# Attention and gated MLP, one core: every transpose of the attention weights takes all 128 rows of its tile

## The chip, the cores and the metric

The kernel runs on one core of one Trainium2 chip. The metric is the device time of one execution in microseconds (us), the median of several runs.

## The reference

Eight batches of eight heads, 576 tokens, head size 64, so 64 heads in all; then a feed-forward part with spatial gating on each batch.

```python
scores = scale * np.matmul(q, k.transpose(0, 1, 3, 2))
cum = np.cumsum(np.maximum(s, 0.0), axis=-1)
bias = -(cum[:, :, :, None] - cum[:, :, None, :])
scores = np.where(causal, -1000000000.0, scores + np.minimum(bias, 0.0))
attn = np.exp(scores - np.max(scores, axis=-1, keepdims=True))
attn = attn / (np.sum(attn, axis=-1, keepdims=True) + 1e-09)
x = np.matmul(attn, v)                 # then [batch, token, 512]
...
h = gelu(x @ w_in)                     # 1024 wide, halves u and v
v_n = layer_norm(v) * g_ln
v_s = np.einsum('ts,bsd->btd', w_sg, v_n) + b_sg[None, :, None]
out = x + (u * v_s) @ w_out
```

Everything above the diagonal of the attention weights is zero.

## The kernel before

**Attention, one head.** The 576 query tokens are cut into five tiles of rows: tile 0 has 64 rows (tokens 0 to 63), tiles 1 to 4 have 128 each and start at tokens 64, 192, 320 and 448 (`IT0`, `ITR`). Only columns up to the tile's last token are computed (`ITW` = 64, 192, 320, 448, 576). `scores` issues the score matmuls (`qk_part`, lines 287 to 290), the masked copy from PSUM with its running minimum on VectorE (`ttr`, line 297), the exponential on ScalarE (`exp_`, line 307) and the division by the row sums (`norm`, line 321, on GpSimd; for the first twelve heads tile 3's is on VectorE). The results are the SBUF tiles p_0 to p_4; two sets of them (`pbuf`) serve even and odd heads. Columns right of `ITW` up to the padded width `PW` are cleared once at the start and stay zero.

`transposes` then turns these weights, 128 key columns at a time, into PSUM. A transpose is a TensorE matmul whose stationary operand is the block of p and whose moving operand is the identity `ident`, all fp32 (line 362, in one place 402). It goes through four banks of PSUM a head, taken from the pool `ps_pt` of two buffers:

- bank A, key tokens 0 to 127: tiles 3, 2, 1 and 0;
- bank B, tokens 256 to 383 for tiles 2, 3 and 4, and tile 4's tokens 0 to 127;
- bank C, tokens 128 to 255: tiles 1 to 4;
- bank D, tokens 384 to 511 for tiles 3 and 4, and tile 4's last 64 tokens.

In each of the banks B, C and D one tile meets the diagonal with half its rows: its first 64 rows hold only zeros there. For this block `half=True` transposes rows 64 to 127 alone, that is a 64-row block that starts at partition 64. Tile 0 has 64 rows anyway. So each head has five transposes of 64 rows (one in each of A, B and C, two in D) and ten of 128.

After each bank the PSUM tile is copied out by `evac`: from head 12 on as a high part (ScalarE, a rounding copy at line 85) and a low part (VectorE, the rest, line 90), pah and pal and so on; before that as one plain copy (line 374). `pv` multiplies these with the values (lines 438, 443, 455; its first bank x0 also comes from `ps_pt`).

**Feed-forward.** `ffn` runs for one batch while the next batch's heads are in work: matmuls at lines 494 (vm), 556 (um), 571 to 575 (sm) and 590 (om), each sum of products of high and low parts.

**Order.** Each step has a place on an axis counted in heads, and steps are issued by place. The framework's scheduler then lays the instructions of every engine in an order of its own, so neighbours on a queue are its choice.

Of the kernel before, what the change touches and what calls it, by code (L numbers as in the profile page):

```python
# [8 lines left out]
F32 = mybir.dt.float32  # L9
# [5 lines left out]
ALU = mybir.AluOpType  # L15
# [5 lines left out]
P = 128  # L21
# [10 lines left out]
ITR = [64, 128, 128, 128, 128]  # L32
ITW = [64, 192, 320, 448, 576]
PW = [128, 256, 384, 512, 576]
# [22 lines left out]
def tile_attn_gmlp(  # L57
# [12 lines left out]
    nc = tc.nc  # L70
# [9 lines left out]
    def eng(key):  # L80
        return [{"s": nc.scalar, "g": nc.gpsimd, "v": nc.vector}[x] for x in ENG[key]]
# [10 lines left out]
    heads = {}  # L92
# [25 lines left out]
            with later():  # L118
                nc.sync.dma_start(out=d["vr"], in_=vp[h])

# [1 line left out]
    dram = ctx.enter_context(tc.tile_pool(name="dram", bufs=1, space=bass.MemoryType.DRAM))  # L122
    cum = dram.tile([2, BH, S], F32, name="cum")
    st = moe.tile([P, 5, BH], F32, name="st", tag="vt", bufs=2)
# [9 lines left out]
    for c0, n in ((0, 512), (512, REM)):  # L134
        ps = ps_sc.tile([P, 512], F32, name="cps", tag="sc")
# [14 lines left out]
    split(cc[0:BH, 0, :], cc[0:BH, 1, :], cf[0:BH, :], nc.scalar, nc.gpsimd)  # L150
    nc.sync.dma_start(out=cum.rearrange("a h s -> h a s"), in_=cc[0:BH].bitcast(F32))

# [1 line left out]
    ident = const.tile([P, P], F32, name="ident")  # L154
    nc.vector.memset(ident, 0.0)
    nc.gpsimd.affine_select(out=ident, in_=ident, pattern=[[1, P]], base=0, channel_multiplier=-1,
# [5 lines left out]
    half = const.tile([P, 1], F32, name="half")  # L162
    nc.vector.memset(half, -0.5)
    g_b = const.tile([P, DH], F32, name="g_b")

# [1 line left out]
    q2 = []  # L167
    pbuf = []
    sums = []
    for i in range(2):  # L170
        t = const.tile([66, S], F32R, name=f"q2_{i}")
        nc.vector.memset(t[64:66, :].bitcast(F32), 1.0)
        q2.append(t)
        ts_ = []
        for it in range(5):
            t = const.tile([P, PW[it]], F32, name=f"p_{i}_{it}")
            if PW[it] > ITW[it]:
                nc.gpsimd.memset(t[:, ITW[it]:PW[it]], 0.0)
            ts_.append(t)
        pbuf.append(ts_)  # L180
        t = const.tile([P, 5], F32, name=f"sum_{i}")
        nc.vector.memset(t, 1.0)
        sums.append(t)

# [1 line left out]
    wi = const.tile([P, NC, 2, DFF], F32R, name="wi")  # L186
    wo = const.tile([P, NC, 2, DM], F32R, name="wo")
    ws = const.tile([P, NT, 2, S], F32R, name="ws")
# [69 lines left out]
                part(wide, w_out[c * P:(c + 1) * P, fs], wo[:, c, 0, fs], wo[:, c, 1, fs])  # L258
                yield 1

# [1 line left out]
    xr = {}  # L262

    def split_head(h):
# [17 lines left out]
    def qk_part(h, it, pst, c0, j0, j1):  # L282
        d = heads[h]
        i0, r = IT0[it], ITR[it]
        o = pst[0:r, c0:c0 + j1 - j0]
        if h < NQ:
            nc.tensor.matmul(o, d["q"][:, i0:i0 + r], d["k"][:, j0:j1], start=True, stop=True)  # L287
            return
        nc.tensor.matmul(o, d["q1"][:, i0:i0 + r], d["k1"][:, j0:j1], start=True, stop=False)  # L289
        nc.tensor.matmul(o, q2[h % 2][:, i0:i0 + r], d["k2"][0:66, j0:j1], start=False, stop=True)  # L290

    def ttr(h, it, pst, c0, j0, j1, first):
        d = heads[h]
        r = ITR[it]
        m0 = 448 + 128 - ITW[it] if it else 448
        mn = d["mn"]
        nc.vector.tensor_tensor_reduce(  # L297
            out=pbuf[h % 2][it][0:r, j0:j1], in0=pst[0:r, c0:c0 + j1 - j0],
            in1=mask[0:r, m0 + j0:m0 + j1], scale=-0.125,
            scalar=3.0e38 if first else mn[0:r, it:it + 1],  # L300
            op0=ALU.add, op1=ALU.min, accum_out=mn[0:r, it:it + 1])
# [6 lines left out]
                             accum_out=sums[h % 2][0:r, it:it + 1])  # L308

    def norm(h, its, rs):  # L310
        c = slice(its[-1], its[0] + 1)
        nc.vector.tensor_scalar(out=rs[:, c], in0=sums[h % 2][:, c], scalar1=1e-9, scalar2=None, op0=ALU.add)
        nc.vector.reciprocal(out=rs[:, c], in_=rs[:, c])  # L313
        for it in its:
            r, w = ITR[it], ITW[it]
            p = pbuf[h % 2][it][0:r, 0:w]
            e = eng("n0" if h < NP else "n")[it]
            if e is nc.scalar:
                nc.scalar.activation(out=p, in_=p, func=AF.Copy, scale=rs[0:r, it:it + 1])
            else:  # L320
                e.tensor_scalar(out=p, in0=p, scalar1=rs[0:r, it:it + 1], scalar2=1.0, op0=ALU.mult, op1=ALU.mult)  # L321

    def scores(h):
        d = heads[h]
        d["mn"] = att.tile([P, 5], F32, name="mn", tag="mn")
        t = ps_sc.tile([P, 512], F32, name="sc", tag="sc")
        qk_part(h, 3, t, 0, 0, 448)
        qk_part(h, 0, t, 448, 0, 64)
        ttr(h, 3, t, 0, 0, 448, True)
        exp_(h, 3)  # L330
        ttr(h, 0, t, 448, 0, 64, True)
        exp_(h, 0)
        yield 0.5
        t = ps_sc.tile([P, 512], F32, name="sc", tag="sc")
        qk_part(h, 2, t, 0, 0, 320)
        qk_part(h, 1, t, 320, 0, 192)
        ttr(h, 2, t, 0, 0, 320, True)
        exp_(h, 2)
        ttr(h, 1, t, 320, 0, 192, True)
        exp_(h, 1)  # L340
        yield 0.5
        rs = att.tile([P, 5], F32, name="rs", tag="rs")
        norm(h, (3, 2, 1, 0), rs)
        t = ps_sc.tile([P, 512], F32, name="sc", tag="sc")
        qk_part(h, 4, t, 0, 0, CH)
        ttr(h, 4, t, 0, 0, CH, True)
        t = ps_sc.tile([P, 512], F32, name="sc", tag="sc")
        qk_part(h, 4, t, 0, CH, S)
        ttr(h, 4, t, 0, CH, S, False)
        exp_(h, 4)  # L350
        yield 0.6
        norm(h, (4,), rs)
        yield 0.1

    def transposes(h):
        d = heads[h]
        pb = pbuf[h % 2]
        pt = {}

        def tr(ps, c, it, jb, half=False):  # L360
            a, r = (64, 128) if half else (0, ITR[it])
            nc.tensor.transpose(out=ps[:, c:c + r - a], in_=pb[it][a:r, jb:jb + P], identity=ident[a:r, a:r])  # L362

        def new(name, w):
            if h < NP:
                x = "hl"[h % 2]
                pt[name] = (att.tile([P, w], F32, name=name + x, tag=name + x, bufs=1),)
            else:
                pt[name] = tuple(att.tile([P, w], F32R, name=name + x, tag=name + x, bufs=1) for x in "hl")

        def evac(name, c0, ps, w, e=nc.scalar):
            if h < NP:
                o = pt[name][0][:, c0:c0 + w]
                (e.copy if e is nc.scalar else e.tensor_copy)(out=o, in_=ps[:, 0:w])  # L374
            else:
                hi, lo = (t[:, c0:c0 + w] for t in pt[name])
                split(hi, lo, ps[:, 0:w], nc.scalar, nc.vector)

        d["pt"] = pt
        t = ps_pt.tile([P, 512], F32, name="pt", tag="pt")  # L380
        for it in (3, 2, 1, 0):
            tr(t, IT0[it], it, 0)
        new("pa", 896)
        evac("pa", 0, t, 448)
        yield 0.43
        t = ps_pt.tile([P, 512], F32, name="pt", tag="pt")
        tr(t, 128, 2, 256, True)
        tr(t, 192, 3, 256)
        tr(t, 0, 4, 0)
        tr(t, 320, 4, 256)  # L390
        evac("pa", 448, t, 448, nc.vector)
        yield 0.43
        t = ps_pt.tile([P, 512], F32, name="pt", tag="pt")
        tr(t, 0, 1, 128, True)
        for it in (2, 3, 4):
            tr(t, 128 * it - 192, it, 128)
        new("pb", 448)
        evac("pb", 0, t, 448)
        yield 0.43
        t = ps_pt.tile([P, 512], F32, name="pt", tag="pt")  # L400
        tr(t, 0, 3, 384, True)
        nc.tensor.transpose(out=t[0:64, 192:256], in_=pb[4][64:128, 512:576], identity=ident[64:128, 64:128])
        tr(t, 64, 4, 384)
        new("pd", 192)
        if h < NP:
            pe = att.tile([P, 64], F32, name="pe", tag="pe", bufs=1)
            nc.vector.tensor_copy(out=pe[0:64, :], in_=t[0:64, 192:256])
            evac("pd", 0, t, 192, nc.vector)
        else:
            pe = att.tile([P, 64], F32R, name="pe", tag="pe", bufs=1)  # L410
            hi, lo = pt["pd"]
            nc.scalar.copy(out=pe[0:64, :], in_=t[0:64, 192:256])
            nc.scalar.copy(out=hi, in_=t[:, 0:192])
            nc.vector.tensor_tensor(out=pe[64:128, :], in0=t[0:64, 192:256], in1=pe[0:64, :].bitcast(F32),
                                    op=ALU.subtract)
            nc.vector.tensor_tensor(out=lo, in0=t[:, 0:192], in1=hi.bitcast(F32), op=ALU.subtract)
        d["pe"] = pe
        yield 0.35

# [45 lines left out]
        del heads[h]  # L465
        yield 0.5

# [1 line left out]
    def ffn(b):  # L469
        xs = []  # L470
        for c in range(NC):
# [128 lines left out]
        for w in (ORD0 if b == 0 else ORDL if b == B - 1 else ORDER).split():  # L600
            yield from unit[w[0]](int(w[1]), int(w[2:] or 0))

# [1 line left out]
    steps = []  # L604
    tick = count()

# [3 lines left out]
    def advance(g, h):  # L610
        if h not in g[1]:
            g[1][h] = g[0](h)
        next(g[1][h], None)

    sc, tr, pp = (scores, {}), (transposes, {}), (pv, {})
    for h in range(BH):
        if h > 0:
# [79 lines left out]
```

## Time and profile before

| | us |
|---|---|
| median of 3 runs | 873.3 |
| lowest and highest run | 872.01, 875.57 |
| span of the profiled execution, first to last instruction | 869.9 |
| PE busy in it | 849.2 |
| DVE, POOL, ACT busy | 671.3, 567.6, 562.3 |
| weight loads (PEld) busy | 713.6 |

Of the profiled execution the page gives the span; the median of the runs lies 3.4 us above it, the lowest run 2.1 us. PE is TensorE's matmuls, PEld its weight loads, which go beside matmuls. A matmul's row begins when it reads its first data, and its end is modelled; rows of neighbouring matmuls overlap, so the distance from one start to the next tells what one costs, not the length of a row. In a row such as `64*128 64x128` the part with the star is rows*columns of the stationary operand.

### The profile page before, as it was taken

The page shows a single profiled execution, that of the slowest core. Times are in us where ns is not written, and L with a number is a line of the kernel's source. Part 1 is how long each engine was busy: PE and PEld are TensorE (multiplying, and loading weights), DVE is VectorE, ACT ScalarE, POOL GpSimd, SP SyncE. Part 2 cuts the span into 40 slices and gives each one's busy share as a digit, 9 for nine tenths or more (in the row PEclk, how much of TensorE's full clock was granted, in tenths as well). Part 3 has the DMA queues.
Part 4 walks back from the last instruction along what each step waited for, and adds up shares of the span by engine and source line. Part 5 has one row for each costly group of instructions (what it writes and reads, how often), then busy time and mean ns, then how long its engine had stood idle before and what let it go on. Part 6 is the DMA issues. An engine that isn't in the chain of part 4 may idle for free.

```text
span 869.9 us, 17259 instructions
## 1 busy us (share of the span) xinstructions
PE 849.2 (98%) x5341; PEld 713.6 (82%) x5341; DVE 671.3 (77%) x2041; ACT 562.3 (65%) x1544; POOL 567.6 (65%) x885
## 2 busy tenths in 40 slices
PE   6899899999999999999999999999999999999988
PEld 3455567988889888898889988889888988899888
DVE  5998778866798678975899668976789668984662
ACT  4677567766687566865677567875668657872340
POOL 4978747767478557685667666786576855773441
PEclk9999999999999999999999999999999999999999
DMA  7556442344333444434424443434344334310101
GB/s 217 173 161 169 125 126 63 104 111 112 86 96 77 107 115 102 106 88 108 125 65 101 112 119 82 98 92 110 105 110 102 87 98 124 77 29 29 40 7 54
DMA packets 68271, 87.23 MB, mean 100 GB/s; under 512 B 24418, under 2 KB 40676, under 8 KB 68180
## 3 DMA queue, kind: packets, MB, share of 16 engines
q1 hardware_dynamic: 68180, 86.14, 37.7%
q8 instruction: 42, 0.69, 0.4%
q14 instruction: 49, 0.40, 0.2%
HBM read 40.17 MB, written 9.73 MB: 57 GB/s over the span
## 4 chain that ended last, share of the span: by engine, by line
PE 89%; DVE 3%; DMA 2%; ACT 2%; POOL 2%; issue 1%; SPq 0%; DVEq 0%; ACTq 0%
PE pt L362 17%; PE om L590 12%; PE xx L438 12%; PE sm L571 11%; PE um L556 10%; PE vm L494 10%; PE sc L289 5%; PE sc L290 5%; PE sc L287 2%; PE x L443 1%; PE sm L574 1%; PE sm L575 1%; PE vm L509 1%; PE vm L508 1%; DMA kf<-in_kq 1%
## 5 line engine op out<-in xcount | busy, mean ns | idle before, releaser
L321 POOL TENSOR_SCALAR p<-p,rs 128x192 f32<-128x192 f32 (+3 forms) x308 | 168.6, 561 | 89.8 <-DVE rs L313 55.3
L307 ACT ACTIVATE p<-p,mn 128x448 f32<-128x448 f32 (+4 forms) x320 | 178.0, 559 | 7.4 <-DVE mn L297 6.9
L362 PE MATMUL pt<-ident,p 128*128 128x128 f32 (+1 forms) x896 | 180.3, 290 | 1.8 <-DVE pah L374 1.6
L297 DVE CUSTOM_DVE_ANT_0 p<-sc,mask 128x448 f32<-128x448 f32 (+4 forms) x320 | 125.5, 422 | 48.3 <-PE pt L362 30.7
L362 PEld LDWEIGHTS pt<-ident,p 128*128 128x128 f32 (+1 forms) x896 | 103.2, 140 | 63.6 <-issue 26.7
L590 PE MATMUL om<-gt,wo 128*128 128x288 f32 x768 | 129.6, 300 | 0.0
L571 PE MATMUL sm<-ws,vn 128*128 128x288 f32 x768 | 124.8, 300 | 1.8 <-DVE u L481 1.2
L556 PE MATMUL um<-xs,wi 128*128 128x288 f32 x768 | 120.8, 298 | 0.3 <-DVE u L577 0.3
L590 PEld LDWEIGHTS om<-gt,wo 128*128 128x128 f32 x768 | 111.5, 188 | 2.6 <-DVE ot L594 0.3
L571 PEld LDWEIGHTS sm<-ws,vn 128*128 128x128 f32 x768 | 108.2, 188 | 3.7 <-DVE u L481 1.9
L90 POOL TENSOR_TENSOR k<-raw,k 128x576 fp32r<-128x576 f32 x56 | 79.8, 1424 | 47.9 <-ACT k L85 44.6
L556 PEld LDWEIGHTS um<-xs,wi 128*128 128x128 f32 x768 | 108.2, 188 | 2.6 <-DVE u L577 0.5
L494 PE MATMUL vm<-wi,xs 128*128 128x512 f32 x384 | 107.8, 401 | 0.5 <-DVE vt L481 0.4
L289 PE MATMUL sc<-k,q 128*128 128x448 f32 x336 | 99.8, 305 | 0.0
L290 PE MATMUL sc<-k,q 66*128 66x448 f32 x336 | 87.8, 296 | 1.0 <-DMA k<-cum 1.0
L90 DVE TENSOR_TENSOR pal<-pt,pah 128x448 fp32r<-128x448 f32 x104 | 63.7, 616 | 19.1 <-ACT pah L85 19.1
L494 PEld LDWEIGHTS vm<-wi,xs 128*128 128x128 f32 x384 | 68.2, 189 | 11.2 <-DVE vt L481 0.7
L90 POOL TENSOR_TENSOR gt<-u,gt 128x288 fp32r<-128x288 f32 x64 | 51.0, 803 | 34.4 <-ACT gt L85 34.4
L85 ACT CAST pah<-pt 128x448 fp32r<-128x448 f32 x104 | 55.1, 532 | 26.7 <-PE pt L362 24.9
L289 PEld LDWEIGHTS sc<-k,q 128*128 128x128 f32 x336 | 60.6, 181 | 10.1 <-DVE wbits L212 1.4
L90 POOL TENSOR_TENSOR vn<-vt,vn 128x512 fp32r<-128x512 f32 x32 | 41.6, 1301 | 40.0 <-ACT vn L85 39.9
L290 PEld LDWEIGHTS sc<-k,q 66*128 66x128 f32 x336 | 60.4, 181 | 6.5 <-DMA k<-cum 1.2
(150 smaller groups left out, 1768.6 us busy)
## 6 DMA issues: line engine op xcount, KB each, us to landing
q<-k SPq DMA_DIRECT2D x168, 144.0 KB
raw<-in_kq SPq DMA_DIRECT2D x56, 288.0 KB
out_t<-ot SPq DMA_DIRECT2D x64, 144.0 KB
vr<-in_vp SPq DMA_DIRECT2D x52, 160.0 KB
k<-k SPq DMA_DIRECT2D x56, 144.0 KB
wraw<-in_w_in SPq DMA_DIRECT2D x16, 256.0 KB
kf<-in_kq SPq DMA_DIRECT2D x8, 288.0 KB
qf<-in_kq SPq DMA_DIRECT2D x8, 288.0 KB
```

Source lines behind the costliest of these rows:

```text
L90: eng_lo.tensor_tensor(out=lo, in0=src, in1=hi.bitcast(F32), op=ALU.subtract)
L289: nc.tensor.matmul(o, d["q1"][:, i0:i0 + r], d["k1"][:, j0:j1], start=True, stop=False)
L290: nc.tensor.matmul(o, q2[h % 2][:, i0:i0 + r], d["k2"][0:66, j0:j1], start=False, stop=True)
L297: nc.vector.tensor_tensor_reduce(out=pbuf[h % 2][it][0:r, j0:j1], in0=pst[0:r, c0:c0 + j1 - j0], in1=mask[0:r, m0 + j0:m0 + j1], scale=-0.125,
L307: nc.scalar.activation(out=p, in_=p, func=AF.Exp, bias=d["mn"][0:r, it:it + 1], scale=-1.0, accum_out=sums[h % 2][0:r, it:it + 1])
L321: e.tensor_scalar(out=p, in0=p, scalar1=rs[0:r, it:it + 1], scalar2=1.0, op0=ALU.mult, op1=ALU.mult)
L362: nc.tensor.transpose(out=ps[:, c:c + r - a], in_=pb[it][a:r, jb:jb + P], identity=ident[a:r, a:r])
L438: nc.tensor.matmul(xx[0:rows, o0:o1], st(jt), m, **{"start": False, "stop": False, **kw})
L494: nc.tensor.matmul(ps[0:r], xs[c][:, xi, ts_], wi[:, c, wj, fs], start=(n == 0), stop=(n == 11))
L556: nc.tensor.matmul(ps[:, 0:CH], wi[:, c, wj, dt * P:(dt + 1) * P], xs[c][:, xi, cs], start=(n == 0), stop=(n == 11))
L571: nc.tensor.matmul(ps[:, 0:CH], vn[j][:, vi, ds_], ws[:, j, wj, cs], start=(n == 0), stop=False)
L590: nc.tensor.matmul(ps[:, 0:CH], wo[:, c, wj, ms], gt[ch, c][:, gi, :], start=(n == 0), stop=(n == 11))
```

## The change

Every transpose takes all 128 rows of its block. Where a half block stood, the whole one is transposed: its first 64 rows are zero, and the 64 PSUM columns that they become are overwritten by the next transposes of that bank or not read. Tile p_0 is cleared as a whole at the start and keeps zeros in its rows 64 to 127. The transposes of a bank are put so that the wanted columns are written last: in bank A tile 0 (columns 0 to 127) goes ahead of tile 1 (64 to 191), and the divisions follow the same order (3, 0, 2, 1). In bank D tile 4's last 64 key columns become a transpose of 128 rows by 64 columns. The copies out of banks C and D start at column 64.

```diff
             t = const.tile([P, PW[it]], F32, name=f"p_{i}_{it}")
-            if PW[it] > ITW[it]:
+            if it == 0:
+                nc.gpsimd.memset(t, 0.0)
+            elif PW[it] > ITW[it]:
                 nc.gpsimd.memset(t[:, ITW[it]:PW[it]], 0.0)
...
-        c = slice(its[-1], its[0] + 1)
+        c = slice(min(its), max(its) + 1)
...
-        norm(h, (3, 2, 1, 0), rs)
+        norm(h, (3, 0, 2, 1), rs)
...
-        def tr(ps, c, it, jb, half=False):
-            a, r = (64, 128) if half else (0, ITR[it])
-            nc.tensor.transpose(out=ps[:, c:c + r - a], in_=pb[it][a:r, jb:jb + P], identity=ident[a:r, a:r])
+        def tr(ps, c, it, jb, n=P):
+            nc.tensor.transpose(out=ps[0:n, c:c + P], in_=pb[it][:, jb:jb + n], identity=ident)
...
-        for it in (3, 2, 1, 0):
+        for it in (3, 0, 2, 1):
             tr(t, IT0[it], it, 0)
...
-        tr(t, 128, 2, 256, True)
+        tr(t, 64, 2, 256)
         tr(t, 192, 3, 256)
         tr(t, 0, 4, 0)
         tr(t, 320, 4, 256)
...
-        tr(t, 0, 1, 128, True)
-        for it in (2, 3, 4):
-            tr(t, 128 * it - 192, it, 128)
+        for it in (1, 2, 3, 4):
+            tr(t, 128 * it - 128, it, 128)
         new("pb", 448)
-        evac("pb", 0, t, 448)
+        evac("pb", 0, t[:, 64:512], 448)
...
-        tr(t, 0, 3, 384, True)
-        nc.tensor.transpose(out=t[0:64, 192:256], in_=pb[4][64:128, 512:576], identity=ident[64:128, 64:128])
-        tr(t, 64, 4, 384)
+        tr(t, 0, 3, 384)
+        tr(t, 256, 4, 512, 64)
+        tr(t, 128, 4, 384)
+        t, te = t[:, 64:256], t[0:64, 320:384]
```

The order on the engines moves with it. Rows give the line, the operation, out<-in by the program's names and rows x columns of the output (so a transpose of 64 rows reads 128x64 here); in the changed kernel the line numbers from the transposes on are three higher, those of the scores and divisions two. First TensorE's queue at banks A of one odd head in the middle (p_..158 to 152 are p_3 to p_0 of that head, sc the scores of the next). Before:

```order
L438 MATMUL xx<-pe,vs 128x64
L362 MATMUL pt<-ident,p_3_158 128x128
L362 MATMUL pt<-ident,p_2_156 128x128
L362 MATMUL pt<-ident,p_1_154 128x128
L362 MATMUL pt<-ident,p_0_152 128x64
L289 MATMUL sc<-k_4339,q_4341 128x448
L290 MATMUL sc<-k_4340,q_1_150 128x448
```

And now:

```order
L441 MATMUL xx<-pe,vs 128x64
L365 MATMUL pt<-ident,p_3_158 128x128
L365 MATMUL pt<-ident,p_0_152 128x128
L365 MATMUL pt<-ident,p_2_156 128x128
L365 MATMUL pt<-ident,p_1_154 128x128
L593 MATMUL om<-gt,wo 128x288 x6
L559 MATMUL um<-xs,wi 128x288 x12
L291 MATMUL sc<-k_4339,q_4341 128x448
```

The transpose of p_0 moved from last to second, and feed-forward matmuls moved between the bank and the next head's scores. Further on, banks B and C of the same head on TensorE. Before:

```order
L362 MATMUL pt<-ident,p_2_156 128x64
L362 MATMUL pt<-ident,p_3_158 128x128
L362 MATMUL pt<-ident,p_4_160 128x128 x2
L494 MATMUL vm<-wi,xs 128x512 x12
L362 MATMUL pt<-ident,p_1_154 128x64
L362 MATMUL pt<-ident,p_2_156 128x128
L362 MATMUL pt<-ident,p_3_158 128x128
L362 MATMUL pt<-ident,p_4_160 128x128
L438 MATMUL xx<-pah,vs 128x448
```

And now:

```order
L497 MATMUL vm<-wi,xs 128x512 x3
L365 MATMUL pt<-ident,p_2_156 128x128
L365 MATMUL pt<-ident,p_3_158 128x128
L365 MATMUL pt<-ident,p_4_160 128x128 x2
L365 MATMUL pt<-ident,p_1_154 128x128
L365 MATMUL pt<-ident,p_2_156 128x128
L365 MATMUL pt<-ident,p_3_158 128x128
L365 MATMUL pt<-ident,p_4_160 128x128
L497 MATMUL vm<-wi,xs 128x512 x9
```

Here the two banks have come to stand side by side, with no matmul between them. Last GpSimd's queue at the divisions of that head (rs_3981 holds its reciprocals; gt is a low part for the o matmuls, xs one for the next batch's input, k2 and vs low parts of coming heads). Before:

```order
L321 TENSOR_SCALAR p_1_3_158<-p_1_3_158,rs_3981 128x448
L321 TENSOR_SCALAR p_1_2_156<-p_1_2_156,rs_3981 128x320
L321 TENSOR_SCALAR p_1_1_154<-p_1_1_154,rs_3981 128x192
L321 TENSOR_SCALAR p_1_0_152<-p_1_0_152,rs_3981 64x64
L90 TENSOR_TENSOR gt_3959<-u2_3418,gt_3959 128x288
L90 TENSOR_TENSOR k2_4340<-raw_4053,k1_4339 128x576
```

And now:

```order
L323 TENSOR_SCALAR p_1_3_158<-p_1_3_158,rs_3981 128x448
L323 TENSOR_SCALAR p_1_0_152<-p_1_0_152,rs_3981 64x64
L323 TENSOR_SCALAR p_1_2_156<-p_1_2_156,rs_3981 128x320
L323 TENSOR_SCALAR p_1_1_154<-p_1_1_154,rs_3981 128x192
L90 TENSOR_TENSOR k2_4340<-raw_4053,k1_4339 128x576
L323 TENSOR_SCALAR p_1_4_160<-p_1_4_160,rs_3981 128x576
L90 TENSOR_TENSOR vs_3940<-vr_3731,vs_3940 128x5x64
L87 TENSOR_SCALAR xs_4212<-xr_3529 128x576
L90 TENSOR_TENSOR xs_4212<-xr_3529,xs_4212 128x576
L90 TENSOR_TENSOR gt_3959<-u2_3418,gt_3959 128x288
```

The division of p_0 moved to second place, and the split into gt_3959 moved behind the two pieces of xs_4212.

More of the change, by code (lines that the diff above doesn't have):

```diff
@@ L406, in transposes @@
             pe = att.tile([P, 64], F32, name="pe", tag="pe", bufs=1)
-            nc.vector.tensor_copy(out=pe[0:64, :], in_=t[0:64, 192:256])
+            nc.vector.tensor_copy(out=pe[0:64, :], in_=te)
             evac("pd", 0, t, 192, nc.vector)
@@ L411, in transposes @@
             hi, lo = pt["pd"]
-            nc.scalar.copy(out=pe[0:64, :], in_=t[0:64, 192:256])
-            nc.scalar.copy(out=hi, in_=t[:, 0:192])
-            nc.vector.tensor_tensor(out=pe[64:128, :], in0=t[0:64, 192:256], in1=pe[0:64, :].bitcast(F32),
+            nc.scalar.copy(out=pe[0:64, :], in_=te)
+            nc.scalar.copy(out=hi, in_=t)
+            nc.vector.tensor_tensor(out=pe[64:128, :], in0=te, in1=pe[0:64, :].bitcast(F32),
                                     op=ALU.subtract)
-            nc.vector.tensor_tensor(out=lo, in0=t[:, 0:192], in1=hi.bitcast(F32), op=ALU.subtract)
+            nc.vector.tensor_tensor(out=lo, in0=t, in1=hi.bitcast(F32), op=ALU.subtract)
         d["pe"] = pe
```

## Prediction

> **What bounds the kernel now.** I read the page's busy shares first, then the chain of work that ended last, then the span cut into stretches, and last single weight loads around the transposes. Busy time and chain:
>
> ```profile
> PE 849.2 (98%) x5341; PEld 713.6 (82%) x5341; DVE 671.3 (77%) x2041; ACT 562.3 (65%) x1544; POOL 567.6 (65%) x885
> ...
> PE 89%; DVE 3%; DMA 2%; ACT 2%; POOL 2%; issue 1%; SPq 0%; DVEq 0%; ACTq 0%
> PE pt L362 17%; PE om L590 12%; PE xx L438 12%; PE sm L571 11%; PE um L556 10%; PE vm L494 10%; PE sc L289 5%; PE sc L290 5%; PE sc L287 2%; PE x L443 1%; PE sm L574 1%; PE sm L575 1%; PE vm L509 1%; PE vm L508 1%; DMA kf<-in_kq 1%
> ```
>
> The 98% alone says little, since a busy matmul row may be one that drains. The second line says more: 89% of the chain is TensorE, and the largest single line in it is the transpose, L362, with 17% of 869.9 us = 148 us. By stretches (busy us of PE, weight loads, DVE, ACT, POOL):
>
> ```profile
> 50.00:100.00 50.00, 47.77 (x216) 26.87 (x214) 44.33 (x143) 35.94 (x106) 42.00 (x54) 0.97 0.58 155
> ...
> 400.00:450.00 50.00, 50.00 (x317) 43.19 (x315) 39.59 (x118) 33.84 (x89) 34.31 (x56) 1.00 0.42 106
> ...
> 800.00:850.00 50.00, 46.91 (x298) 42.22 (x297) 29.54 (x62) 19.04 (x40) 22.37 (x42) 1.00 0.09 24
> ```
>
> In the middle TensorE is full, weight loads fill 86% of it, and the next engine, DVE, is at 79%. In the first 100 us the weight loads are at half of that while DVE and POOL are high, so there TensorE also waits for others. After 800 us no transpose is left (the last one starts at 799 us).
>
> **Where the transposes lose time.** The weight loads by form, with the idle time of the load path just before each form in the last column:
>
> ```profile
> L362 PEld LDWEIGHTS pt<-ident,p 128*128 128x128 f32 x640 | 69.4, 141 | 15.8 <-DVE p L321 0.2
> ...
> L362 PEld LDWEIGHTS pt<-ident,p 64*128 64x128 f32 x256 | 33.8, 136 | 47.7 <-issue 26.7 <-DVE rs L313 3.1 <-DVE pal L90 3.0
> ...
> L402 PEld LDWEIGHTS pt<-ident,p 64*64 64x64 f32 x64 | 6.9, 109 | 0.0
> ```
>
> The form before the shape is rows*columns of the stationary operand. A full 128-row load is preceded by 15.8/640 = 25 ns of idle, a 64-row load by 47.7/256 = 186 ns, and most of that has no releaser ("issue"). The 64*64 load, which always follows a 64-row load, has none. So it is not 64 rows as such that cost, but going from 128 rows to 64. The same in single rows, the first transposes of one head (three full ones, then the 64-row one of tile p_0, then a score matmul):
>
> ```profile
> 414.31 0.31 PEld L362 LDWEIGHTS pt<-ident,p 128*128 128x128 f32 x3
> 414.79 0.14 PEld L362 LDWEIGHTS pt<-ident,p 64*128 64x128 f32 x1 [0.17 <-issue]
> 415.00 0.19 PEld L289 LDWEIGHTS sc<-k,q 128*128 128x128 f32 x1
> 415.10 0.19 PEld L290 LDWEIGHTS sc<-k,q 66*128 66x128 f32 x1
> ```
>
> The three full loads end at 414.62; the 64-row load starts 0.17 us later; the load after it again starts 0.07 us after its end, where loads of 128 and 66 rows overlap each other (415.00 and 415.10, 0.19 us each). The load path stands still on entering the 64-row form and on leaving it.
>
> **The change, part by part.** In time on the chain, from the same stretch (start, us, what):
>
> ```profile
> 414.48 0.58 PE pt L362 x4
> 415.07 0.40 PE sc L289
> ...
> 417.93 0.68 PE pt L362 x4
> ...
> 421.39 0.68 PE pt L362 x4
> 422.07 0.20 PE xx L438
> ...
> 423.72 0.20 PE pt L362
> 423.92 0.06 PE pt L402
> 423.98 0.26 PE pt L362
> 424.24 0.49 PE xx L438 x3
> ```
>
> These are the four banks of one head; call them A to D. The L289 matmul after A takes 0.40 us and not the 0.20 that L438, as wide (448 columns), takes after C: leaving the 64-row form costs 0.20 there, so A costs 0.58 + 0.20 = 0.78. B and C cost 0.68 each, D 0.20 + 0.06 + 0.26 = 0.52. One head: 2.66 us, of it 2.40 on L362 as charged in the chain; 64 x 2.40 = 154 us, against 148 us that the chain holds of that line. So 96% of the transposes' time lies on the path that sets the end.
>
> Now four full transposes. From A (starts and merged lengths of rows that start at each place):
>
> ```profile
> 414.32 0.33 PE L362 MATMUL pt<-ident,p 128*128 128x128 f32 x1
> ...
> 414.32 0.44 PE L362 MATMUL pt<-ident,p 128*128 128x128 f32 x2
> ...
> 414.48 0.38 PE L362 MATMUL pt<-ident,p 128*128 128x128 f32 x2
> ...
> 417.86 0.53 PE L362 MATMUL pt<-ident,p 64*128 64x64 f32 x2
> ...
> 418.06 0.44 PE L362 MATMUL pt<-ident,p 128*128 128x128 f32 x2
> ```
>
> In A the first ends at 414.65 (0.17 after the chain reached it), the second at 414.76, the third at 414.86: one full transpose behind another costs 0.10 to 0.11. In B the first full one starts 0.20 after the 64-row one (418.06 against 417.86). Four full ones cost 0.17 + 3 x 0.11 = 0.50, and the next matmul is charged its usual 0.20.
>
> - Bank A: 0.78 becomes 0.50, saves 0.28 a head. The order inside (3, 0, 2, 1) only keeps the overlapping writes right.
> - Banks B and C: 0.68 becomes 0.50, saves 0.18 each.
> - Bank D: three transposes, the middle one 128 rows by 64 columns. Bounds: 0.17 + 0.06 + 0.11 = 0.34 if the narrow one costs what L402 costs now, and 0.17 + 0.11 + 0.11 = 0.39 if it costs a full one. Saves 0.13 to 0.18; I take 0.16.
> - The moving operand grows from 64 to 128 columns in all five. Price zero, since a transpose is held by its weight load: D's three starts
>
> ```profile
> 423.65 0.27 PE L362 MATMUL pt<-ident,p 64*128 64x64 f32 x1
> 423.76 0.22 PE L402 MATMUL pt<-ident,p 64*64 64x64 f32 x1
> 423.91 0.33 PE L362 MATMUL pt<-ident,p 128*128 128x128 f32 x1
> ```
>
>   put the second 0.11 behind a first that moves 64 columns, as far as full ones lie apart that move 128. If that cover were gone, each would cost at most the 0.05 by which L402's slot (0.15, less the 0.09 of leaving the form) is under a full one's 0.11: 5 x 64 x 0.05 = 16 us, the upper bound.
> - In a few places a 64-row block at partition 0 (p_0) stands right ahead of one at partition 64. There both go side by side, as here, two in the length of one:
>
> ```profile
> 75.29 0.28 PE L362 MATMUL pt<-ident,p 64*128 64x64 f32 x2
> ```
>
>   Seven such pairs in the whole trace; each loses at most one full slot, 7 x 0.11 = 0.8 us, and the two drains around it go. The Trainium skill states the rule behind it (TensorE: Matmul & The Clock Gate, Part 3: Packing small matmuls): a weight load overlaps running matmuls only where its row group differs. By that rule full-row loads could never run ahead, and the change would give up all overlap; the rows above, with loads of 128 and 66 rows 0.10 apart and 0.19 long, disagree, and the sum stands.
> - GpSimd clears two whole p_0 tiles instead of two halves, before the first head: off the chain. Its norm of p_0 moves ahead of those of p_2 and p_1, so these land one 64x64 instruction later; bank A waits for all four in either order. All that the load path idles behind POOL ahead of transposes today (total us, times)
>
> ```profile
>   POOL p L321: 1.3, 8
> ```
>
>   is under 2 us in a launch: zero, and if every one of those waits doubled, 1.3 us.
> - Copies out of PSUM read the same widths from other columns: zero.
>
> Sum: 0.28 + 0.18 + 0.18 + 0.16 = 0.80 us a head, 64 heads: 51 us; on the chain 96% of it: 49 us.
>
> **What comes back.** Two things. Some seven heads have their transposes in the first 100 us, where others set the pace: I count half of 7 x 0.80 = 3 us as lost. And the other engines get 5% less time: DVE goes from 79% to 84% of the middle, so short waits grow. The waits now, in total, times, longest:
>
> ```profile
> ACT pbh L85 <- PE pt L362: 52.2, 39, 3.5
> ...
> DVE p L297 <- PE pt L362: 30.7, 46, 1.7
> ...
> PEld pt L362 <- DVE pal L90: 3.0, 13, 0.3
> ```
>
> ACT and DVE wait for transposes (83 us in these two rows), hardly the reverse (3.0 us): a faster TensorE first eats their waiting. I take 2 us for it. 49 - 3 - 2 = 44 us off the profiled span, 869.9 to 826. The median of the runs, 873.3, is 3.4 above that span; so I say 829 (a difference of 0.5%, 4.4 us, is about what a measurement of this kernel can tell from none).
>
> **The rivals.**
> 1. Half of it is eaten. The scheduler lays all queues anew, with other neighbours; on POOL a `gt` split now stands behind two `xs` pieces. If other engines take back 15 to 30 us in place of the 2 counted, mostly DVE, which in the early stretch above has 44 of 50 us: 829 + 13 to 28 = 842 to 857. Against it: the two long waits on PE above. 17%.
> 2. The narrow transpose drains. 128 rows by 64 columns is a column mode that fp32 transposes don't have yet with 128 rows. If entering and leaving it costs what the row form does (0.09 each, half of B's saving), 64 x 0.18 = 12 us: 829 + 12 = 841. For it: nothing in the rows; against: L402 has 64 columns, too, and 0.06 us and no idle before it. The Trainium skill has a rule that speaks for it (TensorEngine Tiling (Array Packing), Feature Incompatibilities): column tiling excludes the transpose mode for fp32 input. By this trace the 64-column fp32 transpose of L402 shows no such price. 5%.
> 3. Slower: the handover of PSUM banks. Two buffers serve A to D and x0; each is held until ACT's cast (532 ns) and DVE's subtraction (616 ns) are through:
>
> ```profile
> L85 ACT CAST pah<-pt 128x448 fp32r<-128x448 f32 x104 | 55.1, 532 | 26.7 <-PE pt L362 24.9
> ...
> L90 DVE TENSOR_TENSOR pal<-pt,pah 128x448 fp32r<-128x448 f32 x104 | 63.7, 616 | 19.1 <-ACT pah L85 19.1
> ```
>
> Transposes that come faster, and banks B and C that now stand side by side in the queue, ask for the next buffer before it is free, and everything behind waits on TensorE. It decides from 0.80 us of new waiting a head; at a full 0.53 + 0.62 = 1.15 us a head it gives 873.3 + 64 x (1.15 - 0.80) = 896. Against: 3.0 us in all today, seventeen times too little. 3%.
> 4. It doesn't do what it says: the idle before 64-row loads is waiting for p_0 or for a bank, which stays. Then the time is 873 within 4. Against: the gap before them is alike in every bank and has mostly no releaser. 4%.
> 5. More than forecast: the early heads pay in full, banks side by side save their entries (0.17 against 0.11), waits shrink: 873.3 - 51 - 8 = 814 or below. 5%.
>
> **How the numbers follow.** The forecast, a gain of 36 to 54 us, has the remaining 66%: 829, own range 819 to 837. The range that leaves out no more than 2 in 10 runs from rival 5's 814 to 850, which takes in rival 2, the 16 us of hidden columns (829 + 16 = 845) and most of rival 1. Faster: 66 + 17 + 5 + 5 = 93%; same 4%; slower 3%.
>
> **What would show it.** In the trace after: idle before L365's weight loads near 25 ns each for all forms, so the 47.7 us row is gone; bank pieces on the chain at 0.50 and D at 0.34 to 0.39; the matmul behind A at 0.20; L365's share of the chain near 64 x 1.87 / 826 = 14%; DVE near 84% in the middle. The forecast is wrong if a new wait of the weight loads on DVE or ACT of over 10 us appears, if the 64-column form has idle time before or after it, or if pieces are short and the span is not.

## The result, and the profile after

The changed kernel takes 852.35 us (median of 4 runs, 850.25 to 853.12) against 872.65 us: a ratio of 0.9756, 95% interval 0.9724 to 0.9787. It is faster by 2.4%, 20.3 us, where 44 were forecast; 852.35 lies just above the range. The profiled execution has a span of 851.4 us. Its page, busy time and chain:

```profile
PE 808.7 (95%) x5341; PEld 720.2 (85%) x5341; DVE 676.6 (79%) x2041; ACT 558.6 (66%) x1544; POOL 565.2 (66%) x885
...
PE 66%; DVE 17%; ACT 6%; issue 4%; DMA 3%; POOL 3%; SPq 0%; POOLq 0%; ACTq 0%; DVEq 0%
PE sm L574 11%; PE om L593 11%; PE pt L365 9%; PE xx L441 8%; PE vm L497 8%; PE um L559 7%; PE sc L291 4%; PE sc L292 4%; DVE p L299 3%; ACT p L309 2%; DVE rs L314 1%; DVE pal L90 1%; DVE vt L484 1%; PE x L446 1%; DVE vt L535 1%
```

PE is busy 40 us less, where a sum of some 50 us on the transposes was forecast. The chain was 89% TensorE and is now 66%; vector, scalar and issue time have come onto it. Some of what the transposes gave up was taken back as waiting.

The weight loads of the transposes by form, with the idle time before each form:

```profile
L365 PEld LDWEIGHTS pt<-ident,p 128*128 128x128 f32 x896 | 105.8, 142 | 20.1 <-DVE pal L377 4.6 <-POOL p L323 2.1 <-DVE xr L467 2.0
...
L365 PEld LDWEIGHTS pt<-ident,p 128*64 128x64 f32 x64 | 7.1, 111 | 1.2
```

The row with 47.7 us of idle is gone, the full loads idle 20.1/896 = 22 ns each, and the narrow form 1.2/64 = 19 ns: rival 2 (a narrow transpose that drains) did not happen. The waits of the weight loads in the middle (200 to 790 us), in total, times, longest:

```profile
PEld sc L291 <- DVE mn L299: 6.5, 10, 1.7
PEld xx L441 <- ACT pah L85: 4.3, 4, 2.0
PEld pt L365 <- DVE xr L467: 2.0, 2, 1.4
PEld pt L365 <- DVE pal L90: 1.7, 5, 0.4
```

The largest that before had on another engine, from 200 to 800 us, was 3.0 us. In stretches (busy us of PE, weight loads, DVE, ACT, POOL; then clock, DMA share, GB/s):

```profile
150.00:200.00 50.00, 46.65 (x318) 43.54 (x318) 39.53 (x135) 38.22 (x113) 37.20 (x54) 0.93 0.44 108
...
400.00:450.00 50.00, 48.86 (x327) 44.31 (x326) 43.95 (x131) 38.09 (x104) 34.70 (x60) 1.00 0.42 106
...
600.00:650.00 50.00, 48.81 (x329) 44.44 (x327) 46.48 (x137) 38.16 (x103) 34.06 (x59) 1.00 0.44 110
```

In the two later stretches TensorE is no longer full and DVE is at 88 to 93%; others go down to 74%, and from 200 to 750 us as a whole DVE is busy for 457.1 of 550 us, 83%. Between 150 and 200 us even the granted clock (the share of TensorE's full clock that the throttle let through) is down to 0.93.

### The profile page after: what moved, and what is told of

It reads as the page before. It is cut to its first block, busy times and chain, and to the rows that moved or that the text cites. A ratio compares the mean times of both kernels' runs of the same rounds, so it can differ in the third digit from the quotient of the medians.

```text
span 851.4 us, 17310 instructions
## 1 busy us (share of the span) xinstructions
PE 808.7 (95%) x5341; PEld 720.2 (85%) x5341; DVE 676.6 (79%) x2041; ACT 558.6 (66%) x1544; POOL 565.2 (66%) x885
## 4 chain that ended last, share of the span: by engine, by line
PE 66%; DVE 17%; ACT 6%; issue 4%; DMA 3%; POOL 3%; SPq 0%; POOLq 0%; ACTq 0%; DVEq 0%
PE sm L574 11%; PE om L593 11%; PE pt L365 9%; PE xx L441 8%; PE vm L497 8%; PE um L559 7%; PE sc L291 4%; PE sc L292 4%; DVE p L299 3%; ACT p L309 2%; DVE rs L314 1%; DVE pal L90 1%; DVE vt L484 1%; PE x L446 1%; DVE vt L535 1%
## 5 line engine op out<-in xcount | busy, mean ns | idle before, releaser
L323 POOL TENSOR_SCALAR p<-p,rs 128x320 f32<-128x320 f32 (+3 forms) x308 | 164.3, 546 | 52.2 <-DVE rs L315 26.7
L309 ACT ACTIVATE p<-p,mn 64x64 f32<-64x64 f32 (+4 forms) x320 | 178.0, 559 | 27.2 <-DVE mn L299 24.2
L365 PE MATMUL pt<-ident,p 128*128 128x128 f32 (+1 forms) x960 | 149.7, 280 | 10.4 <-DVE pal L377 4.2
L299 DVE CUSTOM_DVE_ANT_0 p<-sc,mask 128x448 f32<-128x448 f32 (+4 forms) x320 | 124.7, 422 | 26.7 <-PE pt L365 13.2
L365 PEld LDWEIGHTS pt<-ident,p 128*128 128x128 f32 (+1 forms) x960 | 111.3, 140 | 21.3 <-DVE pal L377 4.6
L574 PE MATMUL sm<-ws,vn 128*128 128x288 f32 x768 | 127.4, 302 | 1.9 <-DVE u L484 1.2
L559 PE MATMUL um<-xs,wi 128*128 128x288 f32 x768 | 123.5, 300 | 0.3 <-DVE u L580 0.3
L593 PE MATMUL om<-gt,wo 128*128 128x288 f32 x768 | 122.3, 297 | 0.0
L559 PEld LDWEIGHTS um<-xs,wi 128*128 128x128 f32 x768 | 110.2, 190 | 2.7 <-DVE u L580 0.5
L593 PEld LDWEIGHTS om<-gt,wo 128*128 128x128 f32 x768 | 109.4, 188 | 1.8 <-DVE ot L597 0.3
L291 PE MATMUL sc<-k,q 128*128 128x448 f32 x336 | 99.9, 305 | 6.4 <-DVE mn L299 6.2
L292 PE MATMUL sc<-k,q 66*128 66x448 f32 x336 | 90.8, 300 | 0.3 <-DMA k<-cum 0.2
L291 PEld LDWEIGHTS sc<-k,q 128*128 128x128 f32 x336 | 60.8, 182 | 14.8 <-DVE mn L299 10.4
```

The lines of the kernel that those rows point to most:

```text
L299: nc.vector.tensor_tensor_reduce(out=pbuf[h % 2][it][0:r, j0:j1], in0=pst[0:r, c0:c0 + j1 - j0], in1=mask[0:r, m0 + j0:m0 + j1], scale=-0.125,
L309: nc.scalar.activation(out=p, in_=p, func=AF.Exp, bias=d["mn"][0:r, it:it + 1], scale=-1.0, accum_out=sums[h % 2][0:r, it:it + 1])
L365: nc.tensor.transpose(out=ps[0:n, c:c + P], in_=pb[it][:, jb:jb + n], identity=ident)
L559: nc.tensor.matmul(ps[:, 0:CH], wi[:, c, wj, dt * P:(dt + 1) * P], xs[c][:, xi, cs], start=(n == 0), stop=(n == 11))
L574: nc.tensor.matmul(ps[:, 0:CH], vn[j][:, vi, ds_], ws[:, j, wj, cs], start=(n == 0), stop=False)
L593: nc.tensor.matmul(ps[:, 0:CH], wo[:, c, wj, ms], gt[ch, c][:, gi, :], start=(n == 0), stop=(n == 11))
```

## The experiments

In all of them the measure is the ratio to the kernel before, run beside them on the same chip. "Held order" means that the instructions of an engine are chained, at the end of the kernel function, in a written-out list of places taken from the kernel before, instead of as the scheduler lays them. The links only order neighbours on one engine's queue. By the traces they add no wait: e10 below, with the links, has as many semaphore waits in its TensorE queue as the kernel before (1726).

**The change in the old order.** The question is whether the missing 24 us lie in the transposes or in the order that came with them. The changed code, with all five queues held in the order of before:

```diff
+LAID = {'Pool': '0 5+2 3 7+5 ...', 'DVE': ..., 'SP': ..., 'PE': ..., 'Activation': ...}
...
+    for name, text in LAID.items():
+        here = [i for i in fixed[name] if type(i).__name__ not in SKIP]
...
+        for a, b in zip(row, row[1:]):
+            tc.add_manual_dep(here[b], here[a].name, <order only>, reason="laid")
```

> The changed kernel, its instructions laid on every engine in the order that the kernel before has (place for place, by order edges alone; of the transposes inside bank A, by place in the bank). Theory ORDER (the 28 us of new stalls come from the order in which the scheduler laid the changed kernel): the old order brings few of them, so the time is 826 to 836 us, TensorE's weight loads wait for DVE's mn and for sc buffers as little as before, and the chain is again near 89% TensorE. Theory ENGINES (DVE, ACT and POOL simply need that time once TensorE is 50 us shorter, in any order): 846 to 856 us, with the same new waits.

Measured: 836.91 us, ratio 0.9585 (0.9569 to 0.9601), 0.9 us above the range of ORDER and far from that of ENGINES. The same code that took 852.35 us gains 36.5 us in the old order. What ORDER said of the chain did not come:

```profile
PE 69%; DVE 15%; ACT 5%; POOL 4%; issue 3%; DMA 2%; SPq 1%; DVEq 0%; POOLq 0%; ACTq 0%
```

TensorE has 69% of it and not 89%, hardly more than in the changed kernel, though the time is 15.4 us shorter. So the shares of the chain don't tell what an order costs. The chain of e1, at the place where the prediction read the banks of before (start, us, what):

```profile
398.31 0.49 PE pt L373 x4
398.80 0.20 PE sc L299
...
401.46 0.44 PE pt L373 x4
...
404.68 0.44 PE pt L373 x4
405.12 0.20 PE xx L449
...
406.77 0.33 PE pt L373 x3
407.09 0.49 PE xx L449 x3
```

A costs 0.49, B and C 0.44, D 0.33, and the score matmul behind A 0.20. The sum had 0.50, 0.50, 0.50, 0.34 to 0.39 and 0.20.

**The old transposes in the new order.** The reverse: the code of before, with the queues held in the order that the scheduler gave the changed kernel (the same links as above, another list).

> The kernel before (64-row transposes), laid on every engine in the order of the changed kernel. ORDER: the new order costs the old code too, part of it hidden behind the drains: 880 to 895 us. ENGINES: the order is as good as the old one and TensorE, with its drains, is the bound: 868 to 876 us.

Measured: 889.97 us, ratio 1.0190 (1.0175 to 1.0205). So the order alone costs the old transposes 16.6 us and the new ones 852.35 - 836.91 = 15.4 us. The two effects add up: transposes -36.5, order +15 to +17. Cores of e2 (span, clock) and its chain:

```profile
core 0: 888.7 us, clock 0.980
```

```profile
PE 78%; DVE 10%; POOL 3%; issue 3%; DMA 3%; ACT 2%; SPq 0%; POOLq 0%; DVEq 0%; ACTq 0%
```

DVE is on 10% of its chain where it was on 3% of before's, though not one transpose became faster: here the order alone brings the waits. That faster transposes bring DVE onto the chain as well is not excluded by this (15% in e1).

**Only p_0, with 66 rows.** This tells whether the price hangs on 64 rows or on the place of the half blocks: the code of before in the old order, and only the transpose of p_0 in bank A takes 66 rows in place of 64, at partition 0 as before. Bank A and the divisions go in the order 3, 0, 2, 1, p_0 is cleared whole (the links of the order, as above, are not shown again).

```diff
-            a, r = (64, 128) if half else (0, ITR[it])
+            a, r = (64, 128) if half else (0, max(ITR[it], 66))
...
-        norm(h, (3, 2, 1, 0), rs)
+        norm(h, (3, 0, 2, 1), rs)
```

> The kernel before, in its own order laid down by hand, with one part of the change: the transpose of p_0 takes 66 rows and 66 columns in place of 64 and 64 (two rows of zeros; banks B, C and D as before). If a stationary block of 64 rows or fewer is what drains TensorE: bank A falls from 0.78 to 0.50 us of the chain, 64 x 0.28 = 18 us, so 853 to 860 us, and the weight load of p_0 stands behind its neighbour without idle time. If it is the partition at which blocks start, or the number of moving columns, or a wait for p_0 itself: bank A stays at 0.78 and the time at 870 to 875 us.

Measured: 864.46 us, ratio 0.9902 (0.9882 to 0.9923). Its weight loads by form:

```profile
L372 PEld LDWEIGHTS pt<-ident,p 64*128 64x128 f32 x192 | 26.1, 136 | 39.7 <-issue 18.3 <-DVE pah L384 2.9 <-DVE pal L98 2.8
...
L372 PEld LDWEIGHTS pt<-ident,p 66*128 66x128 f32 x64 | 9.1, 142 | 0.8 <-POOL p L331 0.8
```

Two rows more, and the idle before p_0's loads falls to 0.8 us in 64, while the 64-row loads beside it keep 39.7/192 = 0.21 us each. From the starts of its matmuls, bank A with its way out costs 454 ns here and 787 in before. So a block of 64 rows is what drains, as the prediction had read it. The time, though, fell between the two ranges (853 to 860 and 870 to 875): the bank saves what was expected and more, but the kernel gains 8.9 us of the 18. Part of that gap comes with the sequence 3, 0, 2, 1, which is taken up below.

**A shorter VectorE path.** If VectorE, at 95% in parts of the middle, set the pace of e1, taking away one small instruction in each division group should show. The addition of 1e-9 to the row sums is left out (128 instructions), in the new code and in the old, both in the held order.

```diff
-        nc.vector.tensor_scalar(out=rs[:, c], in0=sums[h % 2][:, c], scalar1=1e-9, scalar2=None, op0=ALU.add)
-        nc.vector.reciprocal(out=rs[:, c], in_=rs[:, c])
+        nc.vector.reciprocal(out=rs[:, c], in_=sums[h % 2][:, c])
```

> The changed kernel in the old order, and one VectorE step of each division left out: the reciprocal reads the row sums directly, without the 1e-9 added first (128 instructions of 323 ns, 41 us of VectorE busy time, 0.64 us a head). Theory DVE NEXT (what is still missing of the gain in the middle is VectorE at 95% in the first half of every batch): the stalls there shrink, 827 to 832 us against 836.9. Theory ORDER ONLY (what is missing is still a matter of neighbours, VectorE as such has room): 835 to 838 us.

> The kernel before in its own order, with the same VectorE step left out. Under both theories TensorE with its drains is the bound and VectorE waits for it, so the 41 us of VectorE work are worth 0 to 3 us: 870 to 873 us. A gain of 5 us or more would say that VectorE held the kernel before too, and that the comparison with the changed kernel tells nothing of a new bound.

Measured: 835.0 us, ratio 0.9558 (0.9545 to 0.9571) for the new code, 1.9 us less than e1, as ORDER ONLY has it; 876.71 us, ratio 1.0040 (1.0025 to 1.0054) for the old, slower by 0.4% where a gain of 0 to 3 us was expected. The same stretch of e1 and then of e6:

```profile
400.00:450.00 50.00, 48.99 (x333) 44.86 (x332) 47.54 (x137) 39.78 (x107) 33.09 (x59) 1.00 0.40 103
```

```profile
400.00:450.00 50.00, 48.26 (x329) 44.38 (x328) 47.30 (x130) 39.34 (x106) 33.00 (x60) 1.00 0.38 100
```

Seven instructions fewer on DVE, and it is nearly as busy as before. Over the whole execution the 128 additions held VectorE for 41.9 us in e1, but its busy time falls by only 21.8 us (676.3 to 654.5): a part of a busy VectorE seems to be waiting inside an instruction (more on that at the end). The theory that VectorE's work is the next limit fell; in the middle e6 gains no more on the kernel before than e1 does.

**Which queue's order.** e1 again, but with TensorE's queue alone held; the scheduler lays the other four.

```diff
-LAID = {'Pool': ..., 'DVE': ..., 'SP': ..., 'PE': ..., 'Activation': ...}
+LAID = {'PE': ...}
```

> The changed kernel with the old order laid on TensorE alone; the scheduler lays the other four queues around it as it likes. Theory PE QUEUE (what costs is where transposes stand to the matmuls that need their copies): 836 to 842 us, near the 836.9 of the old order everywhere. Theory OTHER QUEUES (the order on POOL, DVE and ACT costs, as with the split moved on POOL): 846 to 853 us, near the changed kernel.

Measured: 845.94 us, ratio 0.9691 (0.9677 to 0.9705). That is at the lower end of the range of OTHER QUEUES. TensorE's order gives back 6.4 of the 15.4 us; the other 9.0 lie with the other queues, as the scheduler lays them around it.

**The front.** e1 against before, matmul by matmul (TensorE's order is the same, so each matmul has its partner): e1 is only 2.6 us ahead when the twelfth head is through, 36.5 after the last. So e1 again, with the first 12 heads on 64-row blocks.

```diff
+        def half(ps, c, it, jb, n=P):
+            if h >= NP:
+                return tr(ps, c, it, jb, n)
+            a, r = (0, 64) if it == 0 else (64, 128)
+            nc.tensor.transpose(out=ps[0:n, c + a:c + r], in_=pb[it][a:r, jb:jb + n], identity=ident[a:r, a:r])
...
-            tr(t, IT0[it], it, 0)
+            (tr if it else half)(t, IT0[it], it, 0)
...
```

> The changed kernel in the old order, but the first 12 heads keep transposes of 64 rows (placed in the new banks' columns). If TensorE is the bound there too, 12 x 0.80 us are lost: 846 us. If the beginning hides most of what is saved there, as the progress of the two traces says (2.6 us gained by the end of head 12), it is 838 to 840 us.

Measured: 842.36 us, ratio 0.9645 (0.9632 to 0.9658), between the two ranges. The new transposes of the first 12 heads are worth 5.4 us by the medians, of 12 x 0.80 = 9.6. That leaves 5.4 - 2.6 = 2.8 us lost by something else in the front: at the end of head 12 the trace of e9 stands 3.7 us behind before's, with the same 64-row transposes. What differs there in the code is the sequence of the divisions and of bank A's transposes.

**The sequence of the divisions.** The code of before in the held order, with the sequence 3, 0, 2, 1 for the divisions and bank A (e10), and for the divisions alone (e14).

```diff
-        norm(h, (3, 2, 1, 0), rs)
+        norm(h, (3, 0, 2, 1), rs)
...
-        for it in (3, 2, 1, 0):
+        for it in (3, 0, 2, 1):
```

> The kernel before in its own order, with nothing of the change but the sequence 3, 0, 2, 1 of the divisions and of bank A's transposes (64-row blocks as before). Theory FRONT (in the first heads, where TensorE waits for divisions, p_2 and p_1 come one 64x64 division of GpSimd later, 0.3 to 0.5 us a head): 875 to 878 us, lost by head 12. Theory FREE (the sequence costs nothing, as predicted; the kernels with it start slower only by chance): 872 to 874 us.

> The kernel before in its own order, with the sequence 3, 0, 2, 1 for the divisions alone; bank A's transposes stay 3, 2, 1, 0. If late divisions of p_2 and p_1 on GpSimd are what the early heads lose by (4.6 us with both sequences changed), 876 to 879 us. If it is the transpose of p_0 in second place on TensorE, which then waits and holds the queue, 872 to 875 us.

Measured: 878.35 us, ratio 1.0053 (1.0039 to 1.0067), and 878.1 us, ratio 1.0048 (1.0032 to 1.0064). In the traces every queue of e14 holds the instructions of before place for place, but for the divisions on GpSimd; so their sequence alone costs the kernel before about 4 us. Matmul by matmul, e10 loses 5.4 us by head 12 and 1.7 later; e14 loses 2.4 by head 10 and 2.7 later, some 0.5 us in each batch from head 28 on.

In the front most of this is granted clock. The first 120 us of before, e9, e10 and e14 (columns as in the stretches above, the clock third from the end):

```profile
0.00:120.00 120.00, 106.12 (x452) 60.78 (x453) 94.79 (x316) 77.21 (x223) 88.13 (x126) 0.97 0.58 166
```

```profile
0.00:120.00 120.00, 106.47 (x433) 60.03 (x434) 91.02 (x306) 74.21 (x216) 90.08 (x125) 0.94 0.54 160
```

```profile
0.00:120.00 120.00, 105.54 (x423) 59.05 (x423) 94.38 (x305) 73.16 (x213) 87.97 (x125) 0.93 0.54 158
```

```profile
0.00:120.00 120.00, 105.27 (x438) 59.82 (x439) 94.30 (x309) 74.95 (x218) 88.67 (x126) 0.96 0.55 162
```

Against before's 0.97, the missing clock is worth 0.03 x 120 = 3.6 us in e9, which lags by 3.7, 4.8 in e10, which lags by 5.4, and 1.2 in e14, which lags by 2.4. These are single executions; by the mean clock of all executions (0.9916 in e10 and 0.9907 in e14, 0.9929 and 0.9925 in before beside them) the clock takes 1 to 2 of the 4 us. The part in the middle stands in the waits of the weight loads, here of e14 from 200 to 800 us:

```profile
PEld sc L297 <- DVE mn L305: 4.7, 10, 0.8
```

In before the same wait is 1.2 us in 5 times.

**p_0 third.** If the cost is that p_2 and p_1 are divided last, the sequence 3, 2, 0, 1, which also leaves the wanted columns of the bank on top, should get some of it back. In the new code: in the held order (e11), the same with the shorter VectorE path (e12, which leaves out the 1e-9 as e6 does), and as the scheduler lays it (e13).

```diff
-        norm(h, (3, 0, 2, 1), rs)
+        norm(h, (3, 2, 0, 1), rs)
...
-        for it in (3, 0, 2, 1):
+        for it in (3, 2, 0, 1):
```

> The changed kernel in the old order with the sequence 3, 2, 0, 1 in place of 3, 0, 2, 1: p_0 still ahead of p_1, as the overlapping writes need, but p_2 is no longer behind it. FRONT: 2 to 3 us less than the 836.9 of the old order, so 833 to 835 us. FREE: 836 to 838 us.

> Both small steps together on the changed kernel in the old order: the sequence 3, 2, 0, 1, and the reciprocal taken from the row sums without the 1e-9 (which left 835.0). If they add up, 831 to 833 us; if each only shifts the same few waits, 834 to 837 us.

> The changed kernel with the sequence 3, 2, 0, 1, laid by the scheduler as it likes. If the changed kernel's loss is a matter of how the scheduler happens to lay it, any small edit may move it: I expect 846 to 856 us, and the same number as 852.35 within 0.3% if the order it finds stays nearly the same (289 of some 2900 rows of TensorE's queue differ).

Measured: 836.6 us, ratio 0.9574 (0.9561 to 0.9587); 836.76 us, 0.9575 (0.9558 to 0.9593); 853.99 us, 0.9777 (0.9752 to 0.9802). The intervals of the first two overlap those of e1 and e6, that of the last the changed kernel's: the 2 to 3 us of FRONT did not come back. It is shown that moving p_0's division ahead costs about 4 us in the old code; which of the late divisions it hurts stays open.

The best versions are the changed code in the old order: e1 at 0.9585 does the whole computation, 1.7% of the time before better than the change as scheduled (e11, at 0.9574, can't be told from it); e6 at 0.9558 leaves the 1e-9 out.

## Why the forecast was right on the transposes and wrong on the time

- **What bounds the kernel, and the sum of 0.80 us a head: right.** The rows of e1 above repeat the predicted banks within 0.06 us. Over heads 13 to 64 the sum gives 52 x 0.80 = 41.6 us, and e1 gained 33.9. e4, where only bank A is changed, gained 10.3 us over the same heads, of 52 x 0.28 = 14.6. No price of the hidden columns shows: B and C stand at 0.44, under the 0.50 that counted none.
- **The early heads: roughly right in size.** The prediction lost 3 us there, e9 shows a loss of 9.6 - 5.4 = 4.2 over the first 12 heads. It may be more: the executions of e9 ran at a mean clock of 0.991, those of e1 at 0.994, which alone is worth some 2.4 of the 5.4 us. (The weight loads fill 49% of the first 100 us, which is 57% of the middle's 86% and not half of it; nothing in the sum hangs on that.)
- **Norm sequence, "zero": wrong, about 4 us.** The step counted what the load path idles behind POOL ahead of transposes. It did not count that the divisions of the other tiles move back on GpSimd's queue with everything that waits for them; e10 and e14 put a price on that. In the middle it is a longer wait; in the front it is mostly a lower granted clock, and that the sequence is what lowers the clock there is not shown.
- **"I take 2 us for it": wrong, and the largest miss.** The term was for waits that grow because TensorE is faster. The largest waits of the weight loads of e1, 200 to 780 us:

```profile
PEld sc L299 <- DVE mn L307: 4.8, 10, 0.8
PEld xx L449 <- ACT pbh L93: 3.6, 5, 0.7
```

  The first was 1.2 us in before, but e14 has 4.7 of it with the old, slow transposes: it comes with the sequence of the divisions and not with a faster TensorE. The second is not among the rows of before, e10 or e14, and is about the size of the term. The large loss came from elsewhere: some 15 us, because the scheduler laid all queues anew. That was rival 1 ("the scheduler lays all queues anew ... 15 to 30 us in place of the 2 counted"), with its time of 842 to 857 and a chance of 17%. Its reason, DVE short of time, was not the cause: e1 does the same work on DVE in 15.4 us less, and in e2 the cost is there with the old, slow transposes too.
- **The account of the 24 us.** Order, 15.4. Divisions, about 4, as the old code shows it. The rest, some 4 us, was not separated; the second wait above, 3.6 us, is about its size. Over heads 13 to 64 alone e1 lacks 41.6 - 33.9 = 7.7 us of the sum, and the two waits above grew by 3.6 each.
- **"What would show it": half met.** Idle before the loads, as said; bank pieces and the matmul behind A, as said in e1, where they were read. DVE's 83% from 200 to 750 us is near the 84 forecast. The transposes' share of the chain is 9% and not 14. One sign of being wrong came as named: over the whole execution the weight loads' wait on DVE's running minimum (L291 on L299) is 10.4 us, 6.5 of it in the middle. "Pieces are short and the span is not" is the other.

How does an order cost 15 us, when no wait in the table is longer than 2? A part of it is paid twice. The changed kernel around 180 us (stretches as above):

```profile
170.00:180.00 10.00, 6.65 (x45) 5.38 (x43) 8.30 (x29) 8.69 (x27) 8.75 (x13) 1.00 0.43 116
180.00:187.00 7.00, 7.00 (x31) 6.83 (x32) 4.73 (x13) 3.39 (x9) 6.06 (x8) 0.52 0.63 148
187.00:194.00 7.00, 7.00 (x55) 6.83 (x53) 5.56 (x23) 5.16 (x17) 1.33 (x1) 0.99 0.14 35
```

and TensorE's own rows there:

```profile
174.96 0.44 PE L441 MATMUL xx<-pah,vs 128*128 128x448 f32 x1 [1.79 <-ACT pah L85]
...
178.59 0.40 PE L291 MATMUL sc<-k,q 128*128 128x288 f32 x1 [1.34 <-DVE mn L299]
```

Two waits of 1.79 and 1.34 us stand in ten microseconds in which PE is busy for 6.65. In the next seven the granted clock is 0.52 and PE gets 31 matmuls done; in the seven after them, at 0.99, 55. The stall itself costs 10 - 6.65 = 3.3 us, the slow clock behind it another 0.48 x 7 = 3.4. The Trainium skill (TensorE: Matmul & The Clock Gate, Part 1: The HAM clock gate) says that the gate goes to half rate after an idle window of about 3.4 us; the halved clock agrees, but here no single gap was that long, only the busy share of some ten microseconds low. The cores rows of the changed kernel and of e1:

```profile
core 0: 851.4 us, clock 0.988
```

```profile
core 0: 833.4 us, clock 0.996
```

Worked out from them, the missing clock is worth (1 - 0.988) x 851.4 = 10.2 us of full speed in the changed kernel and 0.004 x 833.4 = 3.3 in e1; in e2 it is 0.020 x 888.7 = 17.8 against 0.005 x 869.9 = 4.3 in before. That is 7 of the 15 us and 13.5 of the 17, but these single executions overstate it: those profiled of the changed kernel and of e2 had the lowest clock of their kernels, that of e1 the highest. By the mean clock of all executions (0.990 and 0.994; 0.983 in e2 and 0.994 in before beside it) the missing clock makes about 3 of the 15 us and 10 of the 17. This is an account and not an experiment, since the clock was not varied by itself.

## What to carry to other kernels

Read from single loads and bank pieces, the local gain of an edit can be forecast closely, and here it was. But where a scheduler lays the queues, an edit of the program can draw a new order, and the new order has a price of its own, here a loss of 15 to 17 us, nearly 2% of the time: forecast it as a separate term, and measure it apart by holding the old order. When the order is at hand, keep the edit and lay the old order by hand.

## What the runs showed of the hardware that was not expected

A tiny VectorE instruction can be as long as the GpSimd instructions beside it. The addition of 1e-9 to 128x4 sums, in before (minimum, median, maximum in ns):

```profile
L312 DVE TENSOR_SCALAR rs<-sum x128: 113/155/2469, 18.2 to 782.0; 128x4 f32<-128x4 f32 x64, 128x1 f32<-128x1 f32 x64
```

The median is 155 ns, the longest 2469; in the changed kernel the longest is 3.85 us, and it stands on the chain there (start, us, what), with 1% of the whole for this line:

```profile
284.68 0.36 DVE pdl L419
285.40 3.76 DVE rs L314
289.17 0.20 DVE xr L467
289.41 0.66 PE pt L365 x4
```

The same time on all engines of the changed kernel:

```profile
284.20 4.19 POOL L90 TENSOR_TENSOR xs<-xr,xs 128x576 fp32r<-128x576 f32 x3
...
285.32 3.85 DVE L314 TENSOR_SCALAR rs<-sum 128x4 f32<-128x4 f32 x1
...
288.36 0.78 POOL L90 TENSOR_TENSOR gt<-u,gt 128x288 fp32r<-128x288 f32 x1
...
289.29 0.16 DVE L315 RECIPROCAL rs<-rs 128x4 f32<-128x4 f32 x1
...
289.64 0.64 POOL L323 TENSOR_SCALAR p<-p,rs 128x448 f32<-128x448 f32 x1 [0.51 <-DVE rs L315]
```

GpSimd runs three xs pieces (4.19 us, so about 1.4 each) and a gt back to back, from 284.20 to 289.14; the VectorE instruction starts at 285.32, within the first piece, and ends at 289.17, 0.03 us behind the gt. Of the changed kernel's 12 instructions of this line that took over 400 ns 11, all 20 of before's and 25 of the 26 of e1 end 19 to 34 ns behind the end of a GpSimd instruction. The Trainium skill (SBUF — State Buffer, Who interferes with whom) says that the two engines share one pair of ports, and that whoever has it holds it for the whole instruction; the rows agree, and show besides that one VectorE instruction can last through four GpSimd instructions in a row. It would explain how VectorE can be "95% busy" and gain little from less work, and why it matters where the scheduler puts xs and gt beside the divisions. That the order's 9.0 us outside TensorE's queue come from this was not tested by itself.

Taking work away can also make a kernel slower: e7, the kernel before without 128 small instructions and in its own order, loses 0.4% (0.25 to 0.54), in steps of about 0.7 us at the same place of each batch. Why that place loses was not pursued.
